# Block 0 of a fused attention and FFN kernel: q transposed between the two k, and fewer fill-in products on TensorE

## The chip, the core and the metric

The kernel runs on one core of one Trainium2 chip, in one launch. The metric is the device time of that core in microseconds (us), the median of several runs. Engines have these names in the profile: PE is TensorE (PEld is its loading of weights), DVE is VectorE, ACT is ScalarE, POOL is GpSimd, SP is SyncE. SBUF is the core's working memory, PSUM the memory of eight banks into which TensorE writes.

## The reference

Two steps, one behind the other. First a linear attention with decay, over 4 batches, 8 heads, 768 positions and 64 features per head:

```python
for b in range(nb):                       # blocks of 64 positions
    intra = np.einsum('bhic,bhjc->bhij', qb, kb) * Dmask[None]
    intra = np.einsum('bhij,bhjd->bhid', intra, vb)
    inter = np.einsum('bhid,bhde->bhie', qb * lam_pow[None], kv_state)
    out[:, :, sl] = intra + inter
    kv_state = lam_block[None, :, None, None] * kv_state + np.einsum('bhsd,bhse->bhde', kb_dec, vb)
```

`Dmask` is `lam ** (i - j)` at and below the diagonal, one `lam` for each head. Then the attention's output, as 3072 tokens of 512 features, goes through a gated feed-forward layer (FFN) of 1536 inner features:

```python
gate = 1.0 / (1.0 + np.exp(-(x @ w_gate)))
val = x @ w_val
return (gate * val @ w_out).astype(np.float32)
```

Inputs and output are fp32. The kernel computes its products in bf16 with fp32 sums.

## The kernel before

The 768 positions are cut into `NSTEP` = 6 blocks of `C` = 128. For each block n the attention of all four batches gives `XT[n]`, 512 tokens with the features on the partitions. The FFN of block n follows: 12 feature tiles of 128 (`piece_gv`: the gate products gp from `WG`, the value products vp from `WV`, L553; a tanh on ScalarE, L563; a product on VectorE, L543), then the output products po (`piece_po`, L585), a copy and a store. A list of closures (`plan`) puts the attention of block n+1 between the feature tiles of block n. The order of the instructions on every engine is that of the program text: it is written by hand, and nothing reorders it.

Only block 0 has nothing to hide behind: until its attention is done, TensorE has no FFN product. The change lies there, in the lines from L595 to L636. Block 0 goes like this:

- Loads. k of batches 0 and 1 comes as fp32 (`load_hw`, L164, from the SP and ACT queues, tile `H32`, in the profile "h") and is made bf16 by VectorE (`cast_hw`, L358). All else comes through GpSimd's queue (`load0`, L114, and `load_g`, `load_v`), in this order: q of batches 0 and 1, k of 2 and 3, q of 2 and 3, v, then the weights, feature tile by feature tile.
- `t_0(c, b)`: eight transposes on TensorE put q or k of one batch, features on the partitions, into one PSUM tile ("tq", "tk", L285). The tiles lie in the pool `ps_at` of five banks, or, for k of batches 2 and 3, in `ps_ff` of three.
- `e_q` (L340) and `e_k` (L353) copy such a tile from PSUM to SBUF (`QS`, `KS`), on ScalarE or VectorE.
- `s_0(b)` (L295): 16 small products give the scores of one batch in two PSUM tiles ("sp"); VectorE multiplies each with a mask (L302) into `MT[0, b]`, two instructions a batch.
- `a_0(b, engs)` (L311): 16 small products of v with `MT` give the output of one batch ("op"), which is copied to `XT[0]` (L318).
- `zeros(m)` (L599): m products of a 128x128 with a 128x512 bf16 piece of a tile that is all zeros, into a PSUM tile "zps" that nothing reads. These are fill-ins: they keep TensorE at work where it would otherwise wait, since its clock depends on its activity. 11 of them stand ahead of the first transpose, while k is still on its way; 10 more stand between the pieces of block 0.

Tiling mode in this text means how TensorE's array is divided: the fill-ins use it whole (128x128 in the profile), the transposes in two halves (128*64), scores and outputs in four quarters (64*64).

In SBUF the copies of block 0 have each their own tile of the pool `trsb`, with three buffers for each of `QS` and `KS`.

Of the kernel before, what the change touches and what calls it, by code (L numbers as in the profile page):

```python
# [8 lines left out]
FP32 = mybir.dt.float32  # L9
BF16 = mybir.dt.bfloat16  # L10
AF = mybir.ActivationFunctionType
ALU = mybir.AluOpType
# [4 lines left out]
def kernel(  # L17
# [11 lines left out]
    nc = tc.nc  # L29

    B, H, S, D = q.shape
    C = 128
    NSTEP = S // C
    HP = H // 2
    DM = H * D
# [11 lines left out]
    trsb = ctx.enter_context(tc.tile_pool(name="trsb", bufs=3))  # L47
# [27 lines left out]
    def swapped(n, b):  # L75
        return n > 0 and b >= NB2
# [7 lines left out]
    def rows_of(u):  # L84
        return slice(u * 64, (u + 1) * 64)
# [67 lines left out]
    ST, CP, XD = {}, {}, {}  # L153
# [50 lines left out]
    lamq, lamqs = lamq2[:, 0], lamq2[:, 1]  # L204
# [15 lines left out]
    def powers(w):  # L220
        nc.scalar.activation(mask0[:, w], mask0[:, w], AF.Exp)
# [47 lines left out]
    QS, KS, MT, XT, SP, OP = {}, {}, {}, {}, {}, {}  # L269
    QT, KT = {}, {}  # L270
    tqs, tks = {}, {}
# [8 lines left out]
    def t_0(c, b, pool=ps_at, tag="ps"):  # L280
        ps = pool.tile([128, 1, HP, C], BF16, name="t" + c, tag=tag)
        for a in range(2):
            for e in range(2):
                for w in range(2):
                    nc.tensor.transpose(ps[rows_of(w), 0, 2 * a + e, :],  # L285
                                        T_[c, 0][:, b, 2 * (2 * a + w) + e, :], ident)
        (tqs if c == "q" else tks)[0, b] = ps

    def s_0(b):
        sp = [ps_at.tile([128, HP, C], FP32, name=f"sp{w}", tag="ps") for w in range(2)]  # L290
        for a in range(2):
            for e in range(2):
                for w in range(2):
                    for g in range(2):
                        nc.tensor.matmul(sp[w][rows_of(g), 2 * a + e, :],  # L295
                                         lhsT=KS[0, b][rows_of(w), 2 * a + e, rows_of(g)],
                                         rhs=QS[0, b][rows_of(w), 2 * a:2 * a + 2, rows_of(g)],
                                         start=(a == 0 and e == 0), stop=(a == 1 and e == 1),
                                         skip_group_check=True)
        MT[0, b] = mtp.tile([128, 2, HP, C], BF16, tag="MT", name="MT")  # L300
        for w in range(2):
            nc.vector.tensor_tensor(out=MT[0, b][:, w], in0=sp[w], in1=mask0[:, w], op=ALU.mult)  # L302

    def a_0(b, engs):
        n = len(engs)
        ops = [ps_at.tile([128, HP // n, C], FP32, name="op", tag="ps") for _ in range(n)]
        for r in range(HP):
            for e in range(2):
                for g in range(2):
                    o, i = divmod(r, HP // n)  # L310
                    nc.tensor.matmul(ops[o][rows_of(g), i, :], lhsT=T_["v", 0][rows_of(g), b, 2 * r + e, :],  # L311
                                     rhs=MT[0, b][rows_of(g), r % 2, 2 * (r // 2) + e, :],
                                     start=(i == 0 and e == 0), stop=(i == HP // n - 1 and e == 1),
                                     skip_group_check=True)
        if b == 0:
            new_xt(0)
        for o, eng in enumerate(engs):
            (eng.tensor_copy if eng is nc.vector else eng.copy)(  # L318
                XT[0][:, b // 2, o * (HP // n):(o + 1) * (HP // n), b % 2 * C:(b % 2 + 1) * C], ops[o])
# [12 lines left out]
        for bp in range(2):  # L332
            nc.scalar.copy(ST[1, 0][:, bp], cp[bp])

    def e_q(n, bs, eng=None):
        w = len(bs)
        src = tqs[n, bs[0]] if n < FIRST_XBAR else QT[n][:, bs[0]:bs[0] + w]
        t = trsb.tile([128, 2, HP, C], BF16, tag="QS", name="QS")
        if n == 0:
            (nc.scalar.copy if eng is nc.scalar else nc.vector.tensor_copy)(t[:, :w], src)  # L340
        else:
            nc.vector.tensor_tensor(
                out=t[:, :w], in0=src,
                in1=(lamqs if swapped(n, bs[0]) else lamq).unsqueeze(1).to_broadcast([128, w, HP, C]),
                op=ALU.mult)
        for i in range(w):
            QS[n, bs[i]] = t[:, i]

    def e_k(n, bs, parts=1):
        t = trsb.tile([128, 2, HP, C], BF16, tag="KS", name="KS")  # L350
        w = len(bs) // parts
        for i in range(parts):
            nc.scalar.copy(t[:, i * w:(i + 1) * w], tks[n, bs[0]][:, i * w:(i + 1) * w])  # L353
        for i in range(len(bs)):
            KS[n, bs[i]] = t[:, i]

    def cast_hw(b):
        nc.vector.tensor_copy(T_["k", 0][:, b], H32[:, b])  # L358
# [52 lines left out]
    def new_xt(n):  # L411
        XT[n] = xtp.tile([128, 2, NMT, TCH // 2], BF16, tag="XT", name="XT")
# [181 lines left out]

    zps = ps_ff.tile([128, DM], FP32, name="zps", tag="ff")  # L595

    def zeros(m):
        for _ in range(m):
            nc.tensor.matmul(zps, lhsT=ST[1, 0][:, 0, 0], rhs=ST[1, 0][:, 0], start=True, stop=True)  # L599

    exponents(0)
    powers(0)
    exponents(1)
    powers(1)
    zeros(11)
    cast_hw(0)
    cast_hw(1)
    t_0("k", 0)
    e_k(0, [0])
    zeros(1)  # L610
    t_0("k", 1)
    t_0("q", 0)
    e_q(0, [0], nc.vector)
    e_k(0, [1])
    t_0("q", 1)
    e_q(0, [1], nc.scalar)
    zeros(1)
    s_0(0)
    zeros(1)
    s_0(1)  # L620
    for b in range(2, 4):
        t_0("k", b, ps_ff, "ff")
        e_k(0, [b])
    zeros(3)
    for b in range(2, 4):
        t_0("q", b)
        e_q(0, [b], nc.scalar)
    zeros(1)
    s_0(2)
    a_0(0, (nc.scalar,))  # L630
    s_0(3)
    a_0(1, (nc.scalar,))
    zeros(2)
    a_0(2, (nc.scalar,))
    zeros(1)
    a_0(3, (nc.scalar, nc.vector))  # L636


# [183 lines left out]
```

## Time and profile before

| | |
|---|---|
| time, median of 3 runs | 225.48 us (225.28 to 225.75) |
| span of the profiled run | 223.4 us |
| PE busy | 216.8 us, 97% of the span |
| ACT busy | 108.6 us, 49% |
| DVE busy | 103.3 us, 46% |
| POOL busy | 63.7 us, 29% |
| first fill-in starts | 1.53 us |
| first transpose starts | 6.79 us |
| first FFN product of block 0 starts | 15.79 us |
| bf16 fill-in products (zps, L599) | 18 records, 7.1 us busy |

The span is what the profiler sees of the program; a run's time is a little longer. All instants in this text are us from the span's start. An instruction's row in the timeline gives its start, its duration, its engine and line, what it writes and reads with the shapes, and in square brackets how long its engine was idle before it and what ended the wait. Matmuls overlap: one starts long before the one ahead of it ends, so their distance from start to start tells more than their duration. A few matmul records are missing in a trace: 21 weight loads are recorded for the fill-ins, but only 18 products.

### The profile page before, as it was taken

What the parts mean: (1) busy time and instruction counts of PE and PEld (TensorE: products, weight loads), DVE (VectorE), ACT (ScalarE), POOL (GpSimd) and SP (SyncE); (2) the same over time, 40 slices, a digit from 0 to 9 for tenths busy, and PEclk for the clock granted to TensorE, in tenths of its full rate; (3) what the DMA queues carried; (4) which work ended last, traced back from release to release, by engine and by line L of the source; (5) the groups of instructions that cost most, each with busy time, mean ns of one, the idle gap of its engine ahead of it and who ended that gap; (6) DMA issues with size and microseconds to landing.
All of it is one profiled execution on the core that took longest, in us unless ns stands there. A gap on an engine that the chain in (4) does not pass through costs nothing.

```text
span 223.4 us, 5470 instructions
## 1 busy us (share of the span) xinstructions
PE 216.8 (97%) x2310; PEld 107.8 (48%) x2321; DVE 103.3 (46%) x191; ACT 108.6 (49%) x237; POOL 63.7 (29%) x85
## 2 busy tenths in 40 slices
PE   7889999999999999999999999999999999999994
PEld 2465444557444544444544444544444544444443
DVE  4654566439777600785700686700676400333300
ACT  5757774494385523385433376342367342333221
POOL 7999855640291007501920030000000000000000
PEclk9999999999999999999999999999999999999999
DMA  5999999999799987997999986012100012100022
GB/s 115 177 179 187 196 198 183 166 156 169 124 99 157 256 220 110 178 144 163 93 158 179 235 56 42 3 50 94 47 3 0 3 50 94 47 0 1 3 94 95
DMA packets 99401, 25.27 MB, mean 113 GB/s; under 512 B 90032, under 2 KB 96432, under 8 KB 99376
## 3 DMA queue, kind: packets, MB, share of 16 engines
q0 software_dynamic: 77872, 13.90, 77.7%
q1 hardware_dynamic: 20688, 10.69, 19.1%
q10 hardware_dynamic: 816, 0.33, 0.6%
q8 instruction: 18, 0.29, 0.5%
q14 instruction: 7, 0.06, 0.1%
HBM read 28.32 MB, written 6.29 MB: 155 GB/s over the span
## 4 chain that ended last, share of the span: by engine, by line
PE 95%; DMA 2%; issue 1%; DVE 1%; ACT 0%; ACTq 0%; DVEq 0%
PE gp L553 28%; PE po L585 28%; PE vp L553 28%; DMA h<-in_k_dram 2%; PE sp L449 1%; PE cp L509 1%; PE op L473 1%; PE op L487 1%; PE zps L599 1%; PE op L311 1%; PE tk L285 1%; PE sp L295 1%; PE sp L375 0%; PE op L406 0%; PE tq L277 0%
## 5 line engine op out<-in xcount | busy, mean ns | idle before, releaser
L543 DVE SCALAR_TENSOR_TENSOR ht<-sg,vp 128x512 bf16<-128x512 f32 x72 | 49.5, 687 | 93.1 <-PE vp L553 88.5
L553 PE MATMUL gp<-XT,WG 128*128 128x512 bf16 (+1 forms) x296 | 74.3, 374 | 0.0
L553 PE MATMUL vp<-XT,WV 128*128 128x512 bf16 (+1 forms) x296 | 74.3, 373 | 0.0
L563 ACT ACTIVATE sg<-gp 128x512 f32<-128x512 f32 x72 | 43.0, 597 | 59.2 <-PE gp L553 59.2
L585 PE MATMUL po<-WO,ht 128*128 128x512 bf16 (+2 forms) x292 | 63.5, 370 | 0.7 <-issue 0.2
L553 PEld LDWEIGHTS <-WV 128*128 128x128 bf16 x296 | 29.0, 98 | 33.2
L585 PEld LDWEIGHTS <-ht 128*128 128x128 bf16 x300 | 28.3, 98 | 32.2 <-issue 0.4
L553 PEld LDWEIGHTS <-WG 128*128 128x128 bf16 x296 | 28.2, 98 | 31.3
L589 ACT ACTIVATE ob<-po 128x512 f32<-128x512 f32 (+1 forms) x24 | 14.0, 583 | 38.9 <-PE po L585 38.9
L143 ACT ACTIVATE kd<-kb,kds 128x128 bf16<-128x128 bf16 x80 | 25.2, 391 | 0.0
L661 POOL COPY gates<-qt 128x1 bf16<-128x1 bf16 x4 | 0.8, 188 | 48.6 <-DMA qt<-qb 48.6
L499 ACT CAST XT<-op 128x512 bf16<-128x512 f32 x16 | 8.2, 599 | 5.0 <-PE op L487 5.0
L459 DVE TENSOR_TENSOR MT<-sp,mask 128x512 bf16<-128x512 f32 x16 | 10.3, 682 | 0.0
L96 POOL DMA_DIRECT2D vb<-in_v_dram x6 | 9.0, 1504 | 3.2 <-issue 1.6
L102 POOL DMA_DIRECT2D qb<-in_q_dram x10 | 8.8, 891 | 3.4 <-DMA WO<-in_moe_w_out_dram 3.4
L102 POOL DMA_DIRECT2D kb<-in_k_dram x10 | 8.9, 913 | 1.0 <-DMA WG<-in_moe_w_gate_dram 0.6
L599 PE MATMUL zps<-st 128*128 128x512 bf16 x18 | 7.1, 529 | 1.7 <-DVE st L174 1.5
L121 POOL DMA_DIRECT2D WV<-in_moe_w_val_dram x9 | 7.5, 849 | 0.0
L118 POOL DMA_DIRECT2D WG<-in_moe_w_gate_dram x8 | 6.8, 847 | 0.0
L534 DVE SCALAR_TENSOR_TENSOR st<-st,pow_l,cp 128x128 bf16<-128x128 bf16 x24 | 6.7, 342 | 0.0
L96 POOL DMA_DIRECT2D kb<-in_k_dram x5 | 5.9, 1180 | 1.0 <-DMA WG<-in_moe_w_gate_dram 1.0
L353 ACT COPY KS<-tk 128x512 bf16<-128x512 bf16 (+1 forms) x6 | 4.3, 728 | 3.6 <-PE tk L277 2.1
(91 smaller groups left out, 127.2 us busy)
## 6 DMA issues: line engine op xcount, KB each, us to landing
out_dram<-ob SPq DMA_DIRECT2D x19, 256.0 KB, 2.0
vb<-in_v_dram POOLq DMA_DIRECT2D x4, 512.0 KB, 7.1
qb<-in_q_dram POOLq DMA_DIRECT2D x14, 128.0 KB, 7.7
kb<-in_k_dram POOLq DMA_DIRECT2D x12, 128.0 KB, 8.8
WO<-in_moe_w_out_dram POOLq DMA_DIRECT2D x4, 384.0 KB, 12.1
kb<-in_k_dram POOLq DMA_DIRECT2D x5, 256.0 KB, 8.8
qb<-in_q_dram POOLq DMA_DIRECT2D x5, 256.0 KB, 8.4
WG<-in_moe_w_gate_dram POOLq DMA_DIRECT2D x4, 256.0 KB, 6.8
```

What stands on the lines that cost most here:

```text
L96: nc.gpsimd.dma_start(out=T_[c, n][:, b0:nat], in_=src[b0:nat, :, sl, :].rearrange("b h s d -> s (b h) d"))
L102: nc.gpsimd.dma_start(out=T_[c, n][:, m:b1, u::2, :], in_=src[m:b1, 1 - u::2, sl, :].rearrange("b h s d -> s (b h) d"))
L121: nc.gpsimd.dma_start(out=WV[:, :, f0 * 128:f1 * 128], in_=wv_r[:, :, f0 * 128:f1 * 128])
L143: nc.scalar.mul(KD[n][:, at, i, :], T_["k", n][:, at, i, :], kds[:, min(n // FIRST_XBAR, 1), h:h + 1])
L459: nc.vector.tensor_tensor(out=MT[n, bp][:, u], in0=SP[n, bp][u], in1=mask[:, u ^ bp].unsqueeze(1).to_broadcast([128, 2, HP, L]), op=ALU.mult)
L499: nc.scalar.copy(XT[n][:, bp].rearrange("p m (j c i) -> p m j c i", j=2, c=2)[:, :, :, c, :], OP[n, c, bp])
L543: return nc.vector.scalar_tensor_tensor(out=o, in0=g, scalar=1.0, in1=x, op0=ALU.add, op1=ALU.mult)
L553: nc.tensor.matmul(ps[:, part], lhsT=W[:, mt, fs], rhs=XT[n][:, part, mt], start=(part is not second and mt == 0), stop=(part is not first ...
L563: nc.scalar.activation(sg, gp.rearrange("p a b -> p (a b)"), AF.Tanh, scale=0.5)
L585: nc.tensor.matmul(po[:, :c1 - c0], lhsT=HT[n, ft][:, tt * 128:(tt + 1) * 128], rhs=WO[:, ft, c0:c1], start=(ft == 0), stop=(ft == NFT - 1))
L589: (eng.mul if eng is nc.scalar else eng.tensor_scalar_mul)(o, po[:, :c1 - c0], 0.5)
L599: nc.tensor.matmul(zps, lhsT=ST[1, 0][:, 0, 0], rhs=ST[1, 0][:, 0], start=True, stop=True)
```

## The change

It touches the order of block 0 alone:

- q of batch 0 is transposed between k of batch 0 and k of batch 1, and q of batch 1 behind them, with no fill-in among these four. Each has its own PSUM bank, as before.
- The copies of q for batches 0 and 1 are both on VectorE (before: batch 0 on VectorE, batch 1 on ScalarE), those of k and of q for batches 2 and 3 on ScalarE. `e_0` takes the place of `e_q` and `e_k` for block 0, and two batches share one SBUF tile.
- q of batch 3 is transposed and copied behind the scores of batch 2 instead of ahead of them.
- The 11 opening fill-ins become three that read the same zeros as fp32. Of the ten later ones, three stay: two ahead of q of batch 2, one behind it.

What it is for: to take the fill-ins off the chain of work of block 0, and to start each score as soon as its own q and k are there.

```diff
+    def e_0(c, b, eng):
+        es = QS if c == "q" else KS
+        if b % 2 == 0:
+            t = trsb.tile([128, 2, HP, C], BF16, tag=c.upper() + "S", name=c.upper() + "S")
+            for i in range(2):
+                es[0, b + i] = t[:, i]
+        (nc.scalar.copy if eng is nc.scalar else nc.vector.tensor_copy)(
+            es[0, b], (tqs if c == "q" else tks)[0, b][:, 0])
...
-    def zeros(m):
+    nought = ST[1, 0].rearrange("p a h j d -> p (a h j d)").bitcast(FP32)
+
+    def zeros(m, dt=BF16):
+        z = nought if dt is FP32 else ST[1, 0].rearrange("p a h j d -> p (a h j d)")
         for _ in range(m):
-            nc.tensor.matmul(zps, lhsT=ST[1, 0][:, 0, 0], rhs=ST[1, 0][:, 0], start=True, stop=True)
+            nc.tensor.matmul(zps, lhsT=z[:, 0:128], rhs=z[:, 0:DM], start=True, stop=True)
...
-    zeros(11)
+    zeros(3, FP32)
     cast_hw(0)
     cast_hw(1)
     t_0("k", 0)
-    e_k(0, [0])
-    zeros(1)
+    e_0("k", 0, nc.scalar)
+    t_0("q", 0)
+    e_0("q", 0, nc.vector)
     t_0("k", 1)
-    t_0("q", 0)
-    e_q(0, [0], nc.vector)
-    e_k(0, [1])
+    e_0("k", 1, nc.scalar)
     t_0("q", 1)
-    e_q(0, [1], nc.scalar)
-    zeros(1)
+    e_0("q", 1, nc.vector)
     s_0(0)
-    zeros(1)
     s_0(1)
     for b in range(2, 4):
         t_0("k", b, ps_ff, "ff")
-        e_k(0, [b])
-    zeros(3)
-    for b in range(2, 4):
-        t_0("q", b)
-        e_q(0, [b], nc.scalar)
+        e_0("k", b, nc.scalar)
+    zeros(2)
+    t_0("q", 2)
+    e_0("q", 2, nc.scalar)
     zeros(1)
     s_0(2)
+    t_0("q", 3)
+    e_0("q", 3, nc.scalar)
     a_0(0, (nc.scalar,))
     s_0(3)
     a_0(1, (nc.scalar,))
-    zeros(2)
     a_0(2, (nc.scalar,))
-    zeros(1)
     a_0(3, (nc.scalar, nc.vector))
```

More of the change, by code (lines that the diff above doesn't have):

```diff
@@ L333, in c_0, with e_q @@
             nc.scalar.copy(ST[1, 0][:, bp], cp[bp])
-    def e_q(n, bs, eng=None):
+    def e_0(c, b, eng):
[6 more added lines that the diff above has]
+            es[0, b], (tqs if c == "q" else tks)[0, b][:, 0])
+    def e_q(n, bs):
         w = len(bs)
@@ L338, in e_q, with e_k @@
         t = trsb.tile([128, 2, HP, C], BF16, tag="QS", name="QS")
[L339 to L345, printed above, removed]
+        nc.vector.tensor_tensor(
+            out=t[:, :w], in0=src,
+            in1=(lamqs if swapped(n, bs[0]) else lamq).unsqueeze(1).to_broadcast([128, w, HP, C]),
+            op=ALU.mult)
         for i in range(w):
             QS[n, bs[i]] = t[:, i]
-    def e_k(n, bs, parts=1):
+    def e_k(n, bs):
         t = trsb.tile([128, 2, HP, C], BF16, tag="KS", name="KS")
-        w = len(bs) // parts
-        for i in range(parts):
-            nc.scalar.copy(t[:, i * w:(i + 1) * w], tks[n, bs[0]][:, i * w:(i + 1) * w])
+        nc.scalar.copy(t, tks[n, bs[0]])
         for i in range(len(bs)):
```

## The prediction

> **What bounds the kernel now.** I read the page's chain first, to see which engine the end hangs on. Its line by engine:
>
> ```profile
> PE 95%; DMA 2%; issue 1%; DVE 1%; ACT 0%; ACTq 0%; DVEq 0%
> ```
>
> So almost any microsecond by which TensorE's long row of FFN products starts earlier comes off the end, unless a transfer is then late. The change lies in block 0, before that row; so I next read the chain in order of time from 6 to 16.3 us (start, duration, what):
>
> ```profile
> 6.30 0.44 DVE kb L358
> 6.74 0.04 issue
> 6.79 0.41 PE tk L285 x8
> 7.20 0.32 PE zps L599
> 7.52 0.34 PE tk L285 x8
> 7.87 0.45 PE tq L285 x16
> ...
> 10.26 0.75 PE zps L599 x3
> 11.02 0.36 PE tq L285 x8
> 11.38 0.02 issue
> 11.40 0.59 ACT QS L340
> 12.00 0.04 issue
> 12.04 0.47 PE sp L295 x16
> 12.51 0.68 DVE MT L302
> ...
> 14.97 0.32 PE zps L599
> 15.29 0.56 PE op L311 x16
> 15.86 0.54 PE gp L553 x4
> ```
>
> The reader is to see that fill-in products (zps) are links of this chain: they don't fill waits there, work waits behind them. The timeline by engine shows the queues beside it:
>
> ```profile
> 9.13 2.48 DVE L302 TENSOR_TENSOR MT<-sp,mask 128x512 bf16<-128x512 f32 x4 [0.57 <-PE sp L295]
> 10.95 0.64 PE L285 MATMUL tq<-ident,qb 128*64 128x128 bf16 x16
> 12.49 2.48 DVE L302 TENSOR_TENSOR MT<-sp,mask 128x512 bf16<-128x512 f32 x4 [0.88 <-PE sp L295]
> ```
>
> VectorE makes four masked scores in 2.48 us, idles 0.88 us, makes four more; those idle 0.88 us are what an earlier q transpose of batch 2 (now at 10.95) can win. What limits that is the load of q for batches 2 and 3, and, further on, of the first weights; the timeline of GpSimd gives the issues, and the transfers of short windows the time to landing (last number, us):
>
> ```profile
> 4.77 1.39 POOL L114 DMA_DIRECT2D qb<-in_q_dram  x2
> ```
> ```profile
> qb<-in_q_dram POOLq DMA_DIRECT2D x1, 128.0 KB, 4.7
> WV<-in_moe_w_val_dram POOLq DMA_DIRECT2D x1, 128.0 KB, 5.6
> ```
>
> The second q load of those two is issued at 5.44, so it lands at 5.44 + 4.7 = 10.14. In the same way q of batches 0 and 1 lands at 2.07 + 5.1 = 7.17, WG of the first feature tile at 9.01 + 5.6 = 14.6, and WV at 9.77 + 5.6 = 15.4.
>
> **What the Trainium skill says.** "TensorE: Matmul & The Clock Gate", Part 1: the array starts at half clock and goes to full after a free-running window of about 3.4 us of activity; a window without activity drops it again. The trace agrees: fill-ins are 0.43 us apart until the clock rises at 6.04 us, 4.5 us after the first one, and 0.22 us after it. "FP8 and Floating Point Precision", TensorE Precision Notes: true fp32 takes 4 passes. No fp32 product is in this trace. "TensorEngine Tiling (Array Packing)", Key Properties: a change of tiling mode drains the array. The trace agrees: the last pair of transposes starts at 6.98, the fill-in of the other mode only at 7.13, 0.15 us later, where pairs of one mode are 0.056 us apart. So one fill-in between two pieces of another mode costs 0.22 + 0.15 = 0.37 us of TensorE.
>
> **Part 1, the opening fill-in.** 11 bf16 products become 3 fp32 ones of the same columns: by the price of 4 passes, 12 passes for 11. An estimate from it: they start at 1.53 as now and would take 12 x 0.43 = 5.1 us at half clock, to 6.65; with the rise at 6.04, to about 6.35. The k cast that the first transpose waits for ends at 6.74. Bounds: if the 4 passes don't hide their weight loads (0.11 to 0.15 us each), up to 12 x 0.57 = 6.8 us at half clock, to some 7.0 with the rise at 6.04 and 8.3 without; if the product were a single pass, they end at 2.8 and the clock rises later. I take hidden: cost nothing, beside the load of k.
>
> **Part 2, the first four transposes.** Now k0, fill-in, k1 (after the second cast, 7.24), q0, q1. After: k0 at 6.79, q0 at max(6.98 + 0.056, 7.17 + 0.04) = 7.2, k1 at 7.43, q1 at 7.65. The new wait for q's landing has k1 and q1 queued behind it, but k1 couldn't start before 7.29 anyway. From first start to the copy's start a batch takes 7.24 - 6.79 = 0.45 us. VectorE copies q0 from 7.65 to 8.08 (0.42) and q1, now its own and no longer ScalarE's, from 8.10 to 8.52; ScalarE copies k1 from 7.88 to 8.47. The first scores s_0(0) start at 8.13 instead of 8.61, s_0(1) at 8.58 instead of 9.28, and the four MT run from 8.65 to 11.13 instead of 9.13 to 11.61. VectorE's additional copy ends before the first MT can start. Gain so far 0.48 us, but it is not on the path that sets the end, as part 3 shows.
>
> **Part 3, batches 2 and 3.** The k transposes follow s_0(1) at about 8.93 (now 9.63); k's load landed at 8.6. Their two copies on ScalarE run from 9.38 to 10.46. Two fill-ins instead of three end at about 9.95. Now q2 meets the load: 10.14 + 0.05, so 10.2 instead of 10.95. Copy on ScalarE 10.65 to 11.24 (now 11.40 to 11.99); the fill-in after the transposes lies beside it. s_0(2) at 11.28 instead of 12.04: gain 0.76 us. MT of batch 2 from 11.8 to 13.07; VectorE is free from 11.13, so it is the scores that set it. q3 has been moved behind s_0(2): transposes at 11.28 + 0.2 + 0.15 = 11.63, copy 12.08 to 12.67, s_0(3) at 12.71. Now both copies were done before s_0(2), and MT3 was kept by VectorE's queue alone. After, s_0(3)'s scores arrive at 13.2, where VectorE was free at 13.0: the move gives back 0.2 us. MT of batch 3 from 13.2 to 14.5, instead of 13.7 to 14.97. Gain here 0.48.
>
> **Part 4, the last fill-ins.** a_0(0), 12.0 to 12.6, then a_0(1) at 13.1 (its bank comes free with the second MT of batch 2) and a_0(2) at 13.55 lie beside MT3. Before a_0(3) the trace has a fill-in from 14.90, with MT3 done at 14.97: a_0(3) starts 0.25 us late, and its 16 products start within 0.42. Without it, a quarter of a_0(3) needs the first half of MT3 alone and runs from 14.0; the other 12 products start when the second half is there, 14.53, and take 0.31. The mode change adds 0.15: the first FFN product starts at 14.53 + 0.31 + 0.15 = 14.99 instead of 15.79. Gain 0.80 us. WG is there (14.6). The first WV product comes at 15.43, hard behind WV's landing at 15.4, so no wait, but the most that can be won is some 0.84. The XT pieces of batches 2 and 3 end at 14.85 and 15.5, before the second half of the first feature tile at 15.87.
>
> **Does it reach the end?** Everything after keeps its length if no load is late. Nearest: the last WO quarter, issued at 28.23 with 13.9 us to landing, 42.1, is first used at 43.4 and would be at 42.6; WG of the second tile, issued at 10.50, lands at 16.1 and would be used at 16.75. The gain is kept: 225.48 - 0.80 = 224.7 us.
>
> **The rivals.** (A) Something of the front is later than worked out: fp32 fill-ins that run to 7.0 or the clock rising after 8 us, which makes the transposes before it last twice as long. For it: fp32 here is unmeasured and the clock's window is free-running. Against it: q2 waits for its load to 10.2 anyway, with slack of 0.2 us ahead of it. A front later by 0.6 us leaves a gain of 0.80 - (0.6 - 0.2) = 0.4: 225.1, within 0.2%. (B) Slower: the clock does not rise by then or falls back, for want of fill-ins. For it: ten fill-ins of 0.22 us after 6.8 become three, and Part 4 of the clock page says that transposes don't count as TensorE's being busy. Against it: TensorE was busy for only 2.84 of the 3.40 us from 10.2 to 13.6 and kept its clock, and the products s_0 and a_0 stay. If it fell in block 0, some 2.5 us of array work on the path double and the FFN products run at half clock for one more window of 3.4 us, which costs 1.7: some 3 us less the 0.8, so 227.5 us. (C) WV or q lands later than in this trace by 0.3 us: gain 0.5, 225.0; against it, the queue's order ahead of it is unchanged.
>
> **How the numbers follow.** The forecast 0.70 (224.5 to 225.0 with the noise of 0.25 either side that the runs before show), A 0.12, C 0.08, B 0.10. Faster by over 0.2% (below 225.03): the forecast and most of C, 0.77; within 0.2%: A and the rest, 0.13; slower 0.10. The range goes from 224.4 (all gained plus noise) to 225.5, which takes in A and C and leaves out B.
>
> **What would show it.** Right: the clock rises before 7 us, q0 starts at about 7.2, q2 at 10.2 straight after its load, s_0(2) at 11.3, the last MT ends at 14.5, the first gp at 15.0, and VectorE's idle time between the MT groups is 0.6 to 0.7 us. Wrong: a clock below full after 7 us, fp32 fill-ins past 6.8, gaps ahead of vp for WV, or a gp at 15.0 with the same end, which would mean that a later wait took the gain.

## The result, and the profile after

| | before | changed |
|---|---|---|
| time, median of 6 runs | 225.47 us (225.04 to 225.81) | 224.39 us (224.32 to 224.71) |
| ratio, 95% interval | | 0.9954 (0.9941 to 0.9967) |
| the same two once more, another series of runs | 225.03 us | 224.30 us, 0.9966 (0.9953 to 0.9978) |
| span of the first trace | 223.4 us | 222.5 us |
| first FFN product (gp), first and second trace | 15.79, 15.64 us | 15.20, 14.99 us |

The change gains 1.08 us in the first comparison and 0.73 in the second. There are two traces of each kernel; the second ones are called "before_again" and "after_again". In the changed kernel the lines from the old L349 on have moved: L341 is the copy of block 0, L606 the fill-in, L557 the FFN's gp and vp.

The page's chain by engine, changed kernel:

```profile
PE 94%; DMA 2%; DVE 1%; ACT 1%; issue 0%; ACTq 0%; DVEq 0%
```

Its chain in order of time (start, duration, what):

```profile
6.40 0.69 DVE kb L362
7.09 0.04 issue
7.13 0.41 PE tk L285 x8
...
9.39 0.57 PE tk L285 x16
9.96 0.54 PE zps L606 x2
10.49 0.36 PE tq L285 x8
10.86 0.02 issue
10.88 0.59 ACT QS L341
11.47 0.04 issue
11.51 0.42 PE sp L295 x16
...
12.32 0.59 ACT QS L341
12.91 0.04 issue
12.95 0.47 PE sp L295 x16
13.42 1.28 DVE MT L302 x2
14.70 0.04 issue
14.74 0.52 PE op L311 x12
15.27 0.54 PE gp L557 x4
```

Of the fill-ins two are left on it, ahead of q of batch 2 (tq at 10.49). Behind that every link is a transpose, a copy, a score or a mask. The 12 op products that start at 14.74 are three quarters of the last a_0, as the prediction had it: the first quarter needs one half of the mask only.

This trace has a late front: the first cast of k took 0.69 us and not 0.44, and the first transpose came at 7.13 instead of 6.79. In the second trace the first transpose comes at 6.61, and q of batch 2 starts 0.14 us after its load has landed (10.08). The second trace's timeline of VectorE and TensorE:

```profile
8.77 2.48 DVE L302 TENSOR_TENSOR MT<-sp,mask 128x512 bf16<-128x512 f32 x4
...
10.21 0.41 PE L285 MATMUL tq<-ident,qb 128*64 128x128 bf16 x8
...
11.75 2.73 DVE L302 TENSOR_TENSOR MT<-sp,mask 128x512 bf16<-128x512 f32 x4 [0.50 <-PE sp L295]
...
14.53 0.52 PE L311 MATMUL op<-MT,vb 64*64 64x128 bf16 x12 [0.30 <-DVE MT L302]
14.99 0.61 PE L557 MATMUL gp<-XT,WG 128*128 128x256 bf16 x4
15.70 0.61 PE L557 MATMUL vp<-XT,WV 128*128 128x256 bf16 x4
```

Two things are to be seen. The second group of four masked scores takes 2.73 us where the first takes 2.48: 0.25 us of waiting between batch 2 and batch 3. And vp starts 0.71 us after gp, where four products of 256 columns take 0.44: it waited 0.27 us. For what, the transfers of a short window tell; WV of the first feature tile in the first and then in the second trace of the changed kernel (last number: us to landing):

```profile
WV<-in_moe_w_val_dram POOLq DMA_DIRECT2D x1, 128.0 KB, 5.0
```
```profile
WV<-in_moe_w_val_dram POOLq DMA_DIRECT2D x1, 128.0 KB, 6.1
```

Issued at 9.52 and 9.58, they land at 14.5 and 15.7. The second is where vp starts. So in the second trace a part of what block 0 gained is lost again to a load.

### The profile page after: what moved, and what is told of

It is laid out like the page before. It is cut to its first block, busy times and chain, and to the rows that moved or that the text cites. A ratio compares the mean times of both kernels' runs of the same rounds, so it can differ in the third digit from the quotient of the medians.

```text
span 222.5 us, 5457 instructions
## 1 busy us (share of the span) xinstructions
PE 216.2 (97%) x2309; PEld 107.7 (48%) x2309; DVE 104.3 (47%) x192; ACT 108.0 (49%) x236; POOL 64.5 (29%) x85
## 4 chain that ended last, share of the span: by engine, by line
PE 94%; DMA 2%; DVE 1%; ACT 1%; issue 0%; ACTq 0%; DVEq 0%
PE gp L557 28%; PE po L589 28%; PE vp L557 28%; DMA h<-in_k_dram 2%; PE sp L453 1%; PE cp L513 1%; PE op L477 1%; PE op L491 1%; PE tk L285 1%; PE sp L295 1%; DVE MT L302 1%; PE tq L285 1%; ACT QS L341 1%; PE sp L379 0%; PE op L410 0%; PE tq L277 0%
## 5 line engine op out<-in xcount | busy, mean ns | idle before, releaser
L557 PE MATMUL gp<-XT,WG 128*128 128x512 bf16 (+1 forms) x296 | 74.3, 374 | 0.0
L557 PE MATMUL vp<-XT,WV 128*128 128x512 bf16 (+1 forms) x296 | 74.3, 373 | 0.0
L557 PEld LDWEIGHTS <-WV 128*128 128x128 bf16 x296 | 28.9, 98 | 33.2
L557 PEld LDWEIGHTS <-WG 128*128 128x128 bf16 x296 | 28.2, 98 | 31.3
L664 POOL COPY gates<-qt 128x1 bf16<-128x1 bf16 x4 | 1.5, 374 | 50.0 <-DMA qt<-qb 50.0
L102 POOL DMA_DIRECT2D qb<-in_q_dram x10 | 8.8, 892 | 3.1 <-DMA WO<-in_moe_w_out_dram 3.1
L606 PE MATMUL zps<-st 128*128 128x512 f32 (+1 forms) x9 | 5.7, 765 | 1.5 <-DVE st L174 1.5
L96 POOL DMA_DIRECT2D qb<-in_q_dram x5 | 5.8, 1151 | 0.5 <-DMA WO<-in_moe_w_out_dram 0.5
```

The costliest lines, as they stand in the source:

```text
L96: nc.gpsimd.dma_start(out=T_[c, n][:, b0:nat], in_=src[b0:nat, :, sl, :].rearrange("b h s d -> s (b h) d"))
L102: nc.gpsimd.dma_start(out=T_[c, n][:, m:b1, u::2, :], in_=src[m:b1, 1 - u::2, sl, :].rearrange("b h s d -> s (b h) d"))
L557: nc.tensor.matmul(ps[:, part], lhsT=W[:, mt, fs], rhs=XT[n][:, part, mt], start=(part is not second and mt == 0), stop=(part is not first ...
```

## The experiments

Theory A is that of the prediction: the fill-ins on the chain were the cost, and behind them the load of q sets the path. Theory B says that q between the two k is what gains, and theory C that the fill-ins hold the clock. Theory D was formed from the traces: a gap much later, at 115 us, is part of the gain. Each time is a median and is compared with the kernel before in the same series of runs; the last column comes from the run's one trace. "Front to gp" is the time from the first transpose to the first gp; it is 9.00 us in both traces of before.

| run | us | before | ratio (95%) | first transpose, gp, vp |
|---|---|---|---|---|
| before_again | 225.05 | 225.21 | 0.9996 (0.9985 to 1.0006) | 6.64, 15.64, 16.09 |
| old_order_no_fill | 224.36 | 225.21 | 0.9960 (0.9945 to 0.9974) | 6.67, 14.74, 15.79 |
| tail_only | 224.51 | 225.21 | 0.9966 (0.9956 to 0.9977) | 7.14, 15.84, 16.29 |
| q3_ahead | 224.40 | 225.21 | 0.9960 (0.9945 to 0.9976) | 6.90, 14.68, 15.62 |
| before_fp32_open | 224.80 | 225.10 | 0.9991 (0.9983 to 0.9999) | 6.66, 15.66, 16.11 |
| open_bf16 | 224.25 | 225.10 | 0.9963 (0.9949 to 0.9976) | 6.77, 15.02, 15.51 |
| open_one | 225.55 | 225.10 | 1.0016 (1.0006 to 1.0026) | 6.63, 16.56, 17.00 |
| best | 223.96 | 225.10 | 0.9946 (0.9933 to 0.9958) | 6.66, 14.68, 15.71 |
| open_padded | 224.55 | 225.03 | 0.9976 (0.9965 to 0.9986) | 6.64, 15.35, 15.79 |
| after_again | 224.30 | 225.03 | 0.9966 (0.9953 to 0.9978) | 6.61, 14.99, 15.70 |
| gp_first | 224.13 | 225.03 | 0.9956 (0.9943 to 0.9970) | 6.70, 14.99, 15.88 |
| q3_gp_first | 223.99 | 225.03 | 0.9950 (0.9938 to 0.9963) | 6.75, 14.78, 15.79 |

### before_again: the kernel before, unchanged

> The kernel before, once more, for a second trace of it. All theories: ratio 1.000 within 0.0015. If the 0.30 us gap among the po products at 115.4 us of the first trace belongs to the program, it stands here again at the same product and the change removed it somehow; if it is chance, it is gone and the span is about 223.1 us. First gp at 15.8 us either way; if the longer casts of k that the trace of after shows (0.68 and 0.76 us against 0.43 and 0.58) are chance too, they may appear here.

The block-0 chain repeats to the hundredth (9.00 us front to gp). The gap at 115 us is there again, smaller, at the same product: the 24th weight load of this po stage ends a run without gaps, and the 25th is late. TensorE's weight loads in the first and then in the second trace of the kernel before:

```profile
114.50 0.96 PEld L585 LDWEIGHTS <-ht 128*128 128x128 bf16 x5
115.88 1.18 PEld L585 LDWEIGHTS <-ht 128*128 128x128 bf16 x6 [0.42 <-issue]
```
```profile
114.57 0.75 PEld L585 LDWEIGHTS <-ht 128*128 128x128 bf16 x4
115.59 1.39 PEld L585 LDWEIGHTS <-ht 128*128 128x128 bf16 x7 [0.28 <-issue]
```

Between loads lie 0.12 us of idleness as a rule; here 0.42 and 0.28, so the gap is 0.30 and 0.16 us. "Issue" says that the profile shows nothing that TensorE waited for. The long casts of k, which the first trace of the changed kernel has, do not appear here.

### old_order_no_fill: only the fill-ins are taken away

The kernel before, with its order of transposes and copies, and without any fill-in behind the opening ones.

```diff
     e_k(0, [0])
-    zeros(1)
     t_0("k", 1)
...
-    zeros(1)
     s_0(0)
-    zeros(1)
     s_0(1)
...
-    zeros(3)
     for b in range(2, 4):
         t_0("q", b)
         e_q(0, [b], nc.scalar)
-    zeros(1)
     s_0(2)
...
-    zeros(2)
     a_0(2, (nc.scalar,))
-    zeros(1)
     a_0(3, (nc.scalar, nc.vector))
```

> The order and the copies of the kernel before (k0, k1, q0, q1; q2 and q3 ahead of the scores of batch 2), the 11 opening bf16 fill-ins, and none of the ten later ones. Theory A (the fill-ins on the chain were the cost; the load of q for batches 2 and 3 then sets q2; the order of the first four is off the path): q2 straight behind its load at 10.2, s_0(2) at 11.3, MT of batch 3 without an idle time of VectorE ahead of it, first gp at 14.8 to 15.0, time 224.3 to 224.6 us, as fast as after or faster. Theory B (q between the two k is what gains): s_0(2) at 11.7 or later, time 224.9 us or more. Theory C (the fill-ins held the clock): a clock below full in block 0, over 225.5 us.

Its timeline of TensorE:

```profile
10.22 0.64 PE L285 MATMUL tq<-ident,qb 128*64 128x128 bf16 x16 [0.41 <-DMA qb<-in_q_dram]
...
14.74 0.61 PE L553 MATMUL gp<-XT,WG 128*128 128x256 bf16 x4
15.79 0.61 PE L553 MATMUL vp<-XT,WV 128*128 128x256 bf16 x4 [0.44 <-DMA WV<-in_moe_w_val_dram]
```

Theory A holds, B falls: the old order without fill-ins is as fast as the change (0.9960 against 0.9954 and 0.9966), q2 waits for its load, not for anything ahead of it, and gp comes 0.25 us earlier than in after_again. The old order of copies is kept here as well, so q's copies on VectorE are not what gains either. vp then waited for WV: of the 0.90 us by which gp comes earlier than in before_again, vp keeps 0.30.

### tail_only: only the last three fill-ins are taken away

```diff
-    zeros(2)
     a_0(2, (nc.scalar,))
-    zeros(1)
     a_0(3, (nc.scalar, nc.vector))
```

> The kernel before without the fill-ins ahead of a_0 of batches 2 and 3 (three products). Theory A: MT of batch 3 still ends at 14.97; a_0(3) then starts its last 12 products at 15.0 instead of its first at 15.22; first gp at 15.45, gain 0.3 us, 225.15. Theory C or a limit elsewhere: no gain, 225.4 to 225.5.

```profile
15.38 0.52 PE L311 MATMUL op<-MT,vb 64*64 64x128 bf16 x12 [0.30 <-DVE MT L302]
15.84 0.61 PE L553 MATMUL gp<-XT,WG 128*128 128x256 bf16 x4
```

The timeline shows a trace with a late load of k (first transpose at 7.14); front to gp is 8.70 us, 0.30 less than before, as expected. But the time fell by 0.70 us, and its interval (0.52 to 0.99) leaves out 0.3. The gap at 115 us is gone from its trace, which may explain 0.16 to 0.30 of it. The rest, 0.10 to 0.24 us, stays open.

### q3_ahead: q of batch 3 where it was

```diff
     e_0("q", 2, nc.scalar)
+    t_0("q", 3)
+    e_0("q", 3, nc.scalar)
     zeros(1)
     s_0(2)
-    t_0("q", 3)
-    e_0("q", 3, nc.scalar)
```

> After, with q of batch 3 transposed and copied directly behind q of batch 2, ahead of the scores of batch 2 as in the kernel before. Theory A (the move of q3 behind s_0(2) gave back 0.2 us, since MT of batch 3 waits for its scores): VectorE's idle time ahead of the last two MT, 0.15 us in after, is gone, last MT ends 0.15 to 0.2 us earlier, 224.2 us. Rival: the two q copies in a row on ScalarE delay the output copies or q2 itself, no gain, 224.4 to 224.6.

VectorE and TensorE in its timeline:

```profile
11.68 2.48 DVE L302 TENSOR_TENSOR MT<-sp,mask 128x512 bf16<-128x512 f32 x4 [0.54 <-PE sp L295]
...
14.68 0.61 PE L557 MATMUL gp<-XT,WG 128*128 128x256 bf16 x4
15.62 0.61 PE L557 MATMUL vp<-XT,WV 128*128 128x256 bf16 x4 [0.34 <-DMA WV<-in_moe_w_val_dram]
```

The second group of masks takes 2.48 us again, and gp comes at 14.68: the 0.25 us inside are won. All fourteen traces agree with that step. From the first transpose of q2 to gp the kernel before takes 4.84 us; without the last fill-ins it is 4.53 us wherever q3 stays ahead of the scores, and 4.77 or 4.78 wherever it is behind them. The end did not move (224.40), because vp waited for WV until 15.62. So the expectation was right on the step and missed the time.

### before_fp32_open: only the opening fill-in of the change

```diff
-    zeros(11)
+    zeros(3, FP32)
```

> The kernel before with the opening fill-in of the change alone: three fp32 products for 11 bf16 ones, all ten later fill-ins kept. Theory A (hidden beside the load of k): first gp still 9.0 us after the first transpose. Both traces of the kernel before have a gap among the po products at 115.2 to 115.4 us (0.30 and 0.16 us), none of the changed kernels has it. Theory D (it comes from where in TensorE's row of instructions that product stands, and fewer instructions ahead move it): gap gone, 0.15 to 0.3 us faster, 225.0. Rival to D (the gap hangs on when block 0 ends): gap still there, ratio 1.000.

Front to gp is 9.00 us, unchanged, and the gap at 115 us is gone. The time is lower by 0.30 us in the medians; the interval of the ratio reaches from 0.02 to 0.38 us. It speaks for D, thinly.

### open_padded: block 0 of the change, with as many TensorE instructions as before

```diff
-    zeros(3, FP32)
+    zeros(11)
+    for _ in range(7):
+        nc.tensor.matmul(zps[:, 0:32], lhsT=ST[1, 0][:, 0, 0], rhs=ST[1, 0][:, 0, 0, 0, 0:32], start=True, stop=True)
```

> After, with the opening fill-in made of 11 bf16 products as in the kernel before and seven more of 32 columns, so that TensorE's program has as many instructions as that of the kernel before (4644) and block 0 is that of after. Theory D (the gap at 115 us hangs on how many instructions of TensorE lie ahead): a gap of 0.15 to 0.3 us among the po products of the same block at about 114.5, time 224.5 to 224.6. Rival (the gap hangs on when block 0 ends, or is chance): no gap, time as after.

Its weight loads:

```profile
114.28 0.74 PEld L589 LDWEIGHTS <-ht 128*128 128x128 bf16 x4
115.23 1.17 PEld L589 LDWEIGHTS <-ht 128*128 128x128 bf16 x6 [0.20 <-issue]
```

The gap is back at the very same weight load, the 25th of that stage, of 0.08 us here. Of the fourteen traces, the three of programs with 4644 TensorE instructions have it and the eleven others don't. So it hangs on the place in the program, not on when block 0 ends: D holds as to where. That the instructions themselves arrive late there is a guess. How long it is, 0.08 to 0.30 us, varies. In this trace the loads of k and q for batches 2 and 3 also landed 0.35 us later than in after_again (which put gp at 15.35), so the 0.25 us between the two times can't all be laid on the gap.

### open_bf16 and open_one: what the opening fill-in is worth

Both are the changed kernel, with `zeros(12)` and with `zeros(1, FP32)` in place of `zeros(3, FP32)`.

> After, with 12 bf16 opening fill-ins in place of the three fp32 ones. Theory A: fill-ins end at 6.5 us or earlier as in after, nothing on the path changes, time as after, 224.3 to 224.5. Rival (fp32 products hold the clock better, or fewer instructions at the start pay): slower than after by 0.2 us or more.

> After, with one fp32 opening fill-in in place of three: TensorE works from 1.5 to 3.3 us and then waits for k. Theory C (the fill-in is there for the clock, which rises only after a whole window of activity): the clock rises one or two windows later, after 8 us, transposes 0.11 us apart instead of 0.056, first gp 0.5 to 1.5 us later, 224.9 to 226. Rival (the clock rises from the transposes and scores as well, within the first of them): no loss over 0.2 us.

open_bf16 is as fast as the change: fp32 or bf16 makes no difference to the time. Its clock rose only at 7.42 us by the trace's clock record, so that its first transposes still ran at half speed (pairs 0.106 us apart, not 0.056), and gp came at 15.02 all the same. In the changed kernel the timeline has the three fp32 products as six records:

```profile
1.53 4.73 PE L606 MATMUL zps<-st 128*128 128x512 f32 x6 [1.53 <-DVE st L174]
```

From the second on they start 0.853 us apart before the clock rises, which is twice the 0.427 us of a bf16 fill-in. Six of these are twelve passes, the price that the prediction took from the 4 passes of true fp32 in the Trainium skill, "FP8 and Floating Point Precision", TensorE Precision Notes.

The same transposes at full speed, in the timeline of after_again, and then in that of open_one:

```profile
7.32 0.41 PE L285 MATMUL tq<-ident,qb 128*64 128x128 bf16 x8 [0.29 <-DMA qb<-in_q_dram]
7.54 0.42 PE L285 MATMUL tk<-ident,kb 128*64 128x128 bf16 x8
```

```profile
7.24 0.64 PE L285 MATMUL tq<-ident,qb 128*64 128x128 bf16 x8
7.64 0.66 PE L285 MATMUL tk<-ident,kb 128*64 128x128 bf16 x8
...
16.56 0.61 PE L557 MATMUL gp<-XT,WG 128*128 128x256 bf16 x4
```

In open_one eight transposes take 0.40 us to the next eight, not 0.22. Its clock record has the rise at 11.79 us; in the traces with the full opening fill-in that have such a record it lies between 4.43 and 7.42. The gp is 1.57 us later than in after_again, and the time stands at 1.0016 of before against 0.9966 there: some 1.1 us. Against open_bf16, in the same series, it is 1.3 us. The runs of open_one also spread more than those of any other kernel, from 224.85 to 226.22. So C holds for the opening fill-in.

### gp_first, q3_gp_first and best: behind the wait for WV

All put the gate products of all four batches ahead of the value products in the first feature tile of block 0, so that WV is needed 0.44 us later:

```diff
     order = [(gp, WG, first), (vp, WV, first), (gp, WG, second), (vp, WV, second)]
+    if n == 0:
+        order[1], order[2] = order[2], order[1]
```

gp_first is the change with that alone, q3_gp_first has q3_ahead's order as well, and best has q3_ahead's order and no fill-in at all behind the opening ones.

> After, with only the order of the first feature tile changed: gate products of all four batches, then the value products. Theory A: after's vp stands at 15.44, at WV's landing of 14.5 to 15.7; moving vp to 15.9 takes away waits of 0 to 0.25 us: 224.2 to 224.4, not more than 0.15 faster than after. Rival (the order of gp and vp alone is what made best fast): 224.0.

> q3_ahead with the gate products of all four batches ahead of the value products in the first feature tile; its three fill-ins are kept. Theory A (q of batch 3 ahead is worth 0.2 to 0.3 us, and the wait for WV took that in q3_ahead): 224.1 us, 0.25 faster than q3_ahead was; without a wait ahead of vp over 0.1. Rival (q3's place is worth nothing): 224.3 to 224.4, as after.

> q of batch 3 ahead of the scores of batch 2, none of the three remaining fill-ins, and for the first feature tile of block 0 the gate products of all four batches ahead of the value products (they need WV 0.44 us later). In the trace of q3_ahead the first gp came at 14.68 but the first vp waited for WV until 15.62. Theory A (WV's landing is the new bound): gp at 14.6 to 14.8, vp at 15.5 to 15.6 without a wait over 0.1 us, 224.0 us, faster than after by 0.3. Theory C: without any fill-in the clock falls back in block 0, slower than after. Rival: the second gp now waits for the XT piece of batch 3 (DVE until 15.2), which takes back more than 0.2 us.

In one series the change has 224.30, gp_first 224.13 and q3_gp_first 223.99. So the order of the first tile gains 0.17 us, slightly more than the 0.15 that was expected at most, and q3's place another 0.14, less than the expected 0.25. The traces show where the rest went: vp starts 0.88 us after gp in gp_first, but 1.00 us after it in q3_gp_first, right behind WV's landing at 15.74. WV is thus still in the way by 0.12 us, and in best, expected to wait under 0.1, by 0.15. best, in the series before, is at 223.96; measured against the kernel before, it and q3_gp_first differ by less than their intervals, so a cost of the last three fill-ins can no longer be made out. The timeline of TensorE of best:

```profile
10.14 0.64 PE L285 MATMUL tq<-ident,qb 128*64 128x128 bf16 x16 [0.60 <-DMA qb<-in_q_dram]
...
14.68 1.05 PE L557 MATMUL gp<-XT,WG 128*128 128x256 bf16 x8
15.71 1.05 PE L557 MATMUL vp<-XT,WV 128*128 128x256 bf16 x8
```

Block 0 now starts from the load of q and ends on the load of WV. TensorE was idle for 0.60 us ahead of q2, and its products stay at full speed: its eight vp of 256 columns take 0.88 us to the next product, at 16.59, as eight gp do in gp_first. C falls for the fill-ins behind the opening ones.

## Why the prediction was right

The direction and the mechanism were right: the fill-ins were links of the chain, and taking them away moved the FFN's start. The size was 224.7 for 224.39 (and 224.30 in the second comparison): a gain of 0.80 us for 1.08 and 0.73. That the total comes so near is partly luck. Block 0 alone gave 0.59 and 0.65 us in the two pairs of traces, the gap at 115 us, which the prediction did not have, added 0.30 and 0.16, and a wait for WV, which it had ruled out, took 0.27 in the second pair.

- **Part 1, the opening fill-in.** Right in block 0: twelve passes, no cost (before_fp32_open has 9.00 us front to gp). But "cost nothing" was not all: with fewer instructions on TensorE the gap of 0.16 to 0.30 us at 115 us goes. It stood in the trace of before, and I had taken the row of po products for gapless. This is the term that the sum lacked, under "everything after keeps its length".
- **Part 2, the first four transposes.** "Not on the path that sets the end" was right: with the old order the time is the same (old_order_no_fill). In after_again the four MT start at 8.77, predicted 8.65, although k's transposes start at 6.61 instead of 6.79: q0 starts at 7.32, 0.14 us after its load landed, where I had put 0.04. This does not show further on, because q2 waits for its own load. VectorE's idle time between the two groups is 0.50 us for that reason, not the 0.6 to 0.7 forecast.
- **Part 3.** q2 at 10.21 (predicted 10.2), s_0(2) at 11.30 (11.28), the last MT ends 13.80 + 0.68 = 14.48 (14.5). The 0.2 us given back by moving q3 are measured as 0.25 within VectorE's group. So the last fill-ins and q3's move nearly cancel, and almost all that block 0 gained is q2's earlier start.
- **Part 4.** First gp at 14.99 in after_again, predicted 14.99. In the first trace 15.20, since its transposes of k were late by 0.35: rival A in small, though from longer casts and not from the fill-ins. The gain of 0.80 us holds for a first transpose at 6.79, as in the first trace of before. There gp follows the first transpose by 9.00 us, in the changed kernel, as long as k is not late, it follows the load of q; with the first transpose at 6.64, as in before_again, the same sum gives 0.65, and that is what the second pair shows. The last fill-ins alone: 0.30 us by the trace of tail_only, 0.25 by the prediction.
- **WV.** "No wait" was wrong in after_again, by 0.27 us, and gaps ahead of vp were among the signs of being wrong: I took WV's landing, 15.4, as fixed, and it is 14.4 to 15.8. The words "the most that can be won is some 0.84" named the right limit, and q3_ahead and old_order_no_fill run into it.
- **Does it reach the end.** Yes. From the first gp to the end the traces take 207.3 us wherever there is neither the gap nor a wait for WV (after, tail_only, gp_first, before_fp32_open: 207.32 to 207.35).
- **Rival B** did not come. What it feared is real for the opening fill-in (open_one) and not for the later ones (best). Whether the transposes alone would hold the clock is not shown, since other products stand among them in every run.

So the sum for after_again against before_again is: block 0 0.65 us (15.64 to 14.99), the gap 0.16, less 0.27 for WV: 0.54, against 0.48 us between the spans. For the first pair: 0.59 + 0.30 = 0.89, and the spans differ by 0.91.

## What to carry to other kernels

A fill-in for the clock belongs where the engine has nothing to do anyway, here ahead of the first load, and there cutting it to a third cost 1.1 us; between pieces of the chain each costs its own length plus the changes of tiling mode around it. In the trace of before the fill-in at 7.13 stands 0.15 us behind the last transposes and 0.32 ahead of the next, where two pairs of transposes are 0.056 apart: 0.41 us in all, a little more than the 0.37 of the prediction. Before ordering the pieces of a start-up by hand, set the landing times of the loads beside them: here the load of q set the middle and the load of WV the end, so one order of transposes was as good as another, and letting the late load be needed later was worth as much as moving q3. When a short kernel's time moves by a few tenths, look for gaps put down to "issue" far from the edit, at the same instruction in two traces: here one made up about a third of the gain in both pairs of traces.

## What the runs showed of the hardware that was not expected

**One transfer in the row of loads is late, and which one it is moves.** The weights land 0.7 us apart, but between 12 and 17 us one step in each of the fourteen traces is 1.3 to 2.1 us. In each of them a packet of 16 KB of the queue for instructions, 0.97 us long, starts between 12.5 and 14.0 us, and the late load lands 2.0 to 2.25 us after that start: WG at 14.65 for a packet at 12.47 (before), WV at 15.65 for 13.64 (after_again), the second WG at 16.23 for 14.01 (after). That the packet causes it was not tried; it fits all fourteen.

**A cast on VectorE and GpSimd's issuing of transfers seem to stretch each other.** The two casts of k in the timelines of the first traces, before and then after:

```profile
6.30 0.93 DVE L358 CAST kb<-h 128x512 bf16<-128x512 f32 x2 [0.29 <-DMA h<-in_k_dram]
```
```profile
6.40 1.36 DVE L362 CAST kb<-h 128x512 bf16<-128x512 f32 x2 [0.39 <-DMA h<-in_k_dram]
```

In twelve of the fourteen traces the first of these casts takes 0.43 us and the second 0.58 to 0.61. In before they took that, and the v load that GpSimd issued at 6.11 took 0.90 us, where the next one took 0.70; in after the casts took 0.68 and 0.76 and the issue at 6.09 took 0.73. The Trainium skill, "SBUF — State Buffer", Who interferes with whom, has the two engines share a pair of ports, for which VectorE contends in its two-port modes; a cast can enter them, and the engine that issues first blocks the other. These two traces fit the sharing, one engine being the slower in the one and the other in the other. They don't show that the first to issue wins, since GpSimd's issue started first in both, and no run tried it apart. The longer casts are most of the 0.34 us by which the first transpose of the changed kernel came later in the first trace, and its second trace did not have them.
